# Strassen's seven products for the second FFN product of an attention and FFN kernel

## The chip, the core and the metric

The kernel runs on one core of a Trainium2 chip. TensorE (PE) multiplies matrices into PSUM, which has eight banks of 512 float32 columns; VectorE (DVE), ScalarE (ACT) and GpSimd (POOL) do elementwise work, and SyncE (SP) issues the DMAs. Each engine works through a list of instructions in an order that is fixed when the program is built, and semaphores make one engine wait for another. The metric is device time in microseconds.

## The reference

```python
def _attn_ref(q_l, k_l, v_l, q_g, k_g, v_g):          # 8 batches, 8 heads, 512 local and 32 global rows, depth 64
    out_g = sm(scale * q_g @ k_all.T) @ v_all           # global rows see all keys
    s_ll = np.where(abs(i - j) <= 32, scale * q_l @ k_l.T, -1e9)
    a_l = sm(np.concatenate([scale * q_l @ k_g.T, s_ll], -1))
    return np.concatenate([out_g, a_l @ np.concatenate([v_g, v_l], 2)], 2)

def _moe_ref(x, w_in, w_out):                           # x: 4608 x 512, w_in: 512 x 2048, w_out: 2048 x 512
    h = x @ w_in
    g = np.where(h > 0, h, np.exp(np.minimum(h, 0)) - 1)
    return g @ w_out
```

The attention's output, with its heads side by side, is the x of the FFN.

## The kernel before

Float32 products are made of float16 ones: each operand is split into a high and a low half (`xh`, `xl`; `win` and `wout` in two tiles each; `gh`, `gl`), and three products, high by high, high by low and low by high, add up in one PSUM bank.

The FFN works on 17 blocks of 256 rows and, within a block, on eight pairs p of 128 hidden columns. I call one p of one block a step. `ffn1` makes the step's h: 24 matmuls of 256 columns into one bank h of the pool `ps_h` (two banks). ACT then forms Relu (L239) and Exp (L240), POOL the scaled exponential minus one (L241), DVE the maximum of that and the scaled h, which it reads from the bank (L246), ACT casts it to gh (L248), and DVE subtracts to get gl (L249). `ffn2` multiplies gh and gl by the pair's rows of w_out: 12 matmuls of 512 columns into two banks `acc` (128 rows each), which add up over a block's steps and are then scaled by ACT (L284) and stored. `ffn2` of a step is issued when two further steps have had their `ffn1` (`LAG2`).

The first four blocks are done in four parts, "a" to "d", as the weights arrive and are converted; their partial sums go through DRAM. From the fifth block on, group "f", a block runs its eight steps in one pass.

Attention runs beside it. A "slot" is 128 query rows of four heads (or the global rows of four heads), with four stages: scores and row maxima (L458, L469, L472), exponentials on ACT (L476) and their scaling on POOL (L483), transposes on PE (L494) and copies (L497), and the product with v (L516), copied to x (L520). All of these use the pool `ps_a` (four banks). A table `PACE` says how many quarter steps of the FFN (a `yield` of the generator) come with each stage. `defer(n, fn)` puts work n ticks later, where a tick is a quarter step; a scheduler moves some instructions a little after that. After attention only FFN steps are left. `split_x` makes xh and xl of a block ahead; up to `NX` blocks are held.

Of the kernel before, what the change touches and what calls it, by code (L numbers as in the profile page):

```python
# [49 lines left out]
def attn_ffn(ctx: ExitStack, tc: tile.TileContext, qT, qgT, kT, vT, w_in, w_out, mask, out):  # L50
# [28 lines left out]
    def tick():  # L79
        now[0] += 1  # L80
        for fn in later.pop(now[0], []):
            fn()
# [3 lines left out]
            tick()  # L86

    lead = [True]


    msk = wts.tile([P, 3, KW], F32, name="msk")
# [21 lines left out]
    wout = [wts.tile([P, NFT, DM], F16, name=f"wout{k}") for k in "hl"]  # L113
    warm = wout[0][:, NFT - 1, :]
    nc.vector.memset(warm, 0.0)
    for _ in range(WARM):
# [78 lines left out]
    def tables(group):  # L195

        r = slice(*GROUPS[group])
        wm = wts.tile([P, 4], F32, name=f"wm_{group}")
        t = wts.tile([P, NP], F32, name=f"t_{group}")
        kk = wts.tile([P, NP], F32, name=f"kk_{group}")  # L200
        nc.vector.tensor_mul(t[:, r], pww[:, r], pwo[:, r])
        nc.vector.tensor_reduce(out=wm[:, 0:1], in_=t[:, r], op=ALU.max, axis=AX.X)

        def rest():
            all_max(wm[:, 1:2], wm[:, 0:1])
            nc.vector.reciprocal(wm[:, 2:3], wm[:, 1:2])
            nc.vector.tensor_scalar(t[:, r], pwo[:, r], wm[:, 2:3], 16.0, ALU.mult, ALU.mult)
# [5 lines left out]
        defer(5, rest)  # L213


    ready = {}

    def ffn_stream():
# [1 line left out]
        state = {}  # L220

        def ffn1(job, p):
            group, blk, xh, xl, sc = job
            kk = tab[group][2]
            h = ps_h.tile([P, 2, BLK], F32, name="h")
            for j in range(2):
                f = slice((2 * p + j) * P, (2 * p + j + 1) * P)
                k = 0
                for c in range(NC):
                    for wt, xt in ((win[0], xh), (win[0], xl), (win[1], xh)):  # L230
                        nc.tensor.matmul(h[:, j, :], wt[:, c, f], xt[:, c, :], start=k == 0, stop=k == 11)  # L231
# [7 lines left out]
            nc.scalar.activation(g, hf, AF.Relu, scale=sc[:, p:p + 1])  # L239
            nc.scalar.activation(g, g, AF.Exp, scale=-1.0)  # L240
            nc.gpsimd.tensor_scalar(g, g, -1.0, sc[:, NP + p:NP + p + 1], ALU.add, ALU.mult)  # L241
            gh = ffn.tile([P, 2 * BLK], F16, name="gh", bufs=3)
            gl = ffn.tile([P, 2 * BLK], F16, name="gl", bufs=3)

            def elu():
                nc.vector.scalar_tensor_tensor(out=g, in0=hf, scalar=kk[:, p:p + 1], in1=g,  # L246
                                               op0=ALU.mult, op1=ALU.max)
                nc.scalar.copy(gh, g)  # L248
                defer(1, lambda: nc.vector.tensor_sub(gl, g, gh))  # L249

            defer(1, elu)
            pend.append((job, p, gh, gl))
            yield

        def ffn2():
            job, p, gh, gl = pend.pop(0)
            group, blk, _, _, sc = job
            first, last = GROUPS[group][0], GROUPS[group][1] - 1
            if p == first:
                if group == "a":  # L260
                    od[blk] = dram.tile([2, P, DM], F32, name=f"od{blk}")
                state["acc"] = [ps_o.tile([P, DM], F32, name="acc") for _ in range(2)]
                state["o"] = [ffn.tile([P, DM], F32, name="o", bufs=3) for _ in range(2)]
                if group in "bcd":
                    for t in range(2):
                        nc.sync.dma_start(state["o"][t], od[blk][t])
            acc = state["acc"]
            for t in range(2):
                for j in range(2):
                    s = slice(j * BLK + t * P, j * BLK + (t + 1) * P)  # L270
                    f = 2 * p + j
                    for k, (gt, wt) in enumerate(((gh, wout[0]), (gh, wout[1]), (gl, wout[0]))):
                        nc.tensor.matmul(acc[t], gt[:, s], wt[:, f, :], start=p == first and j == 0 and k == 0,  # L273
                                         stop=p == last and j == 1 and k == 2)
                    if j == 0:
                        yield
                if p == last:
                    o = state["o"][t]
                    oc = sc[:, 2 * NP:2 * NP + 1]
                    if group in "bcd":  # L280
                        nc.vector.scalar_tensor_tensor(out=o, in0=acc[t], scalar=oc, in1=o,
                                                       op0=ALU.mult, op1=ALU.add)
                    else:
                        nc.scalar.activation(o, acc[t], AF.Copy, scale=oc)  # L284
                    nc.sync.dma_start(od[blk][t] if group in "abc" else out_rows(blk, t), o)
                yield

        def split_x(blk):
            xr, mx = ready[blk]
# [26 lines left out]
        def scales(group, mx):  # L316
            sc = ffn.tile([P, 2 * NP + 1], F32, name="xs", bufs=4)
            wm, t, _ = tab[group]
            o = GROUPS[group]
            r = slice(*o)  # L320
            nc.gpsimd.tensor_scalar(sc[:, r], isc[:, r], mx[:, 2:3], 1.0, ALU.mult, ALU.mult)
            nc.gpsimd.tensor_scalar(sc[:, NP + o[0]:NP + o[1]], t[:, r], mx[:, 3:4], 1.0, ALU.mult, ALU.mult)
            nc.gpsimd.tensor_scalar(sc[:, 2 * NP:2 * NP + 1], wm, mx[:, 2:3], 2.0 ** -18, ALU.mult, ALU.mult)
            return sc

        order = list(range(NBL + 1))
# [8 lines left out]
        def choose():  # L335

            for blk in order:
                if blk in xs and xs[blk][3] and step[blk] < 4:
                    group = "f" if "f" in tab and not step[blk] else "abcd"[step[blk]]
                    if group in tab:  # L340
                        step[blk] += 4 if group == "f" else 1
                        xh, xl, mx, _ = xs[blk]
                        return group, blk, xh, xl, scales(group, mx)

        job = None
        left = 0
# [258 lines left out]
    for i, _ in enumerate(attention()):  # L605
# [10 lines left out]
        while done < want:  # L616
# [3 lines left out]
            done += 1  # L620
            convert(1)
            tick()
    for _ in f:
        tick()
    drain()
# [57 lines left out]
```

## Time and profile before

| | |
|---|---|
| runs | 1041.33, 1032.25, 1033.97 us; median 1033.97 |
| profiled execution | 1034.22 us; span of the instructions 1032.1 us |
| mean granted TensorE clock | 0.982 |
| busy share | PE 96%, DVE 55%, ACT 51%, POOL 30% |
| DMA | 81.78 MB, 79 GB/s over the span |

A busy share is the time in which an engine had an instruction under way. A group row gives line, engine, operation, what it writes and reads, shape and count, then busy time and mean duration, then the idle time before its instructions and what ended it. In a row of the timeline stand start, length, engine, line and operation.

### The profile page before, as it was taken

The numbers are of one execution on the slowest core, as the hardware profiler recorded it, in microseconds if no ns is written. First come the engines' busy times: TensorE is split into PE (matmuls) and PEld (weight loads), VectorE is DVE, ScalarE is ACT, GpSimd is POOL, SyncE is SP. The second block draws the span as 40 slices with busy tenths as digits, with TensorE's granted clock in tenths as the row PEclk, the third lists the DMA queues.
The fourth block names the chain that finished last, engine by engine and source line by source line (L and its number), as shares of the span: only waits on it lengthen the run. The fifth ranks groups of instructions, "written<-read, shape, count | busy, mean of one in ns | idle before, by whom it ended". The sixth has DMA issues, their size and how long they took to land.

```text
span 1032.1 us, 18890 instructions
## 1 busy us (share of the span) xinstructions
PE 987.5 (96%) x7192; PEld 682.5 (66%) x7192; DVE 565.1 (55%) x1659; ACT 526.6 (51%) x1257; POOL 306.7 (30%) x549
## 2 busy tenths in 40 slices
PE   6899779899999999999999999999999999999996
PEld 4576555566676777766767667667677667666663
DVE  5789698894455555454555445454545454422221
ACT  4778675575344545455544544554545544434342
POOL 3456545344122232223222322232322222211110
PEclk9699899999999999999999999999999999999998
DMA  7546565451321122112310123012200100000000
GB/s 268 160 137 224 180 199 189 159 187 65 108 68 57 43 67 102 32 37 67 98 36 16 42 77 102 27 32 77 97 22 11 42 23 31 1 21 21 1 21 21
DMA packets 39154, 81.78 MB, mean 79 GB/s; under 512 B 3864, under 2 KB 5912, under 8 KB 39064
## 3 DMA queue, kind: packets, MB, share of 16 engines
q1 hardware_dynamic: 39064, 80.58, 23.6%
q8 instruction: 57, 0.93, 0.4%
q14 instruction: 33, 0.27, 0.1%
HBM read 65.36 MB, written 15.20 MB: 78 GB/s over the span
## 4 chain that ended last, share of the span: by engine, by line
PE 84%; DVE 6%; DMA 3%; POOL 2%; ACT 2%; issue 1%; SPq 0%; POOLq 0%; ACTq 0%
PE h L231 32%; PE acc L273 31%; PE pa L516 6%; PE pa L458 5%; PE pa L494 5%; PE pa L406 2%; DVE cu L159 1%; POOL p L483 1%; DMA k<-kT 1%; DVE cu L163 1%; PE acc L458 1%; PE h L516 1%; PE pa L440 1%; ACT p L476 1%; DMA raw<-w_out 1%
## 5 line engine op out<-in xcount | busy, mean ns | idle before, releaser
L231 PE MATMUL h<-xh,winh 128*128 128x256 f16 x1088 | 298.5, 275 | 11.2 <-DVE g L246 5.6
L231 PE MATMUL h<-xh,winl 128*128 128x256 f16 x1088 | 298.1, 274 | 0.0
L231 PE MATMUL h<-xl,winh 128*128 128x256 f16 x1088 | 298.0, 274 | 0.0
L231 PEld LDWEIGHTS <-winh 128*128 128x128 f16 x2176 | 209.8, 98 | 71.0 <-issue 18.7
L241 POOL TENSOR_SCALAR g<-g,xs 128x512 f32<-128x512 f32 x136 | 98.3, 723 | 389.8 <-ACT g L240 356.3
L273 PE MATMUL acc<-wouth,gh 128*128 128x512 f16 x544 | 207.4, 381 | 3.9 <-ACT o L284 2.4
L273 PE MATMUL acc<-woutl,gh 128*128 128x512 f16 x544 | 206.6, 380 | 0.0
L273 PE MATMUL acc<-wouth,gl 128*128 128x512 f16 x544 | 206.3, 380 | 0.0
L483 POOL TENSOR_SCALAR p<-p,sm 128x224 f32<-128x224 f32 x256 | 133.2, 537 | 194.7 <-DVE sm L481 77.8
L246 DVE SCALAR_TENSOR_TENSOR g<-h,kk_f,g 128x512 f32<-128x512 f32 x104 | 78.1, 751 | 195.6 <-POOL g L241 195.2
L248 ACT CAST gh<-g 128x512 f16<-128x512 f32 x136 | 83.8, 617 | 189.3 <-DVE g L246 188.9
L476 ACT ACTIVATE p<-p,m 128x224 f32<-128x224 f32 x256 | 120.1, 470 | 92.0 <-DVE m L472 91.3
L273 PEld LDWEIGHTS <-gh 128*128 128x128 f16 x1088 | 103.4, 98 | 95.8 <-issue 14.3
L239 ACT ACTIVATE g<-h,xs 128x512 f32<-128x512 f32 x136 | 92.7, 682 | 130.0 <-PE h L231 129.8
L249 DVE TENSOR_TENSOR gl<-g,gh 128x512 f16<-128x512 f32 x136 | 95.0, 699 | 46.2 <-ACT gh L248 45.0
L231 PEld LDWEIGHTS <-winl 128*128 128x128 f16 x1088 | 106.9, 98 | 13.9 <-issue 0.6
L273 PEld LDWEIGHTS <-gl 128*128 128x128 f16 x544 | 53.4, 98 | 63.9 <-issue 0.8
L469 DVE CUSTOM_DVE_ANT_0 p<-pa,msk 128x224 f32<-128x224 f32 x228 | 77.3, 384 | 20.1 <-PE pa L458 19.9
L497 DVE COPY pt<-pa 128x512 f32<-128x512 f32 x99 | 67.5, 682 | 36.6 <-PE pa L494 36.2
L240 ACT ACTIVATE g<-g 128x512 f32<-128x512 f32 x136 | 85.2, 628 | 3.4
L494 PE MATMUL pa<-ident,p 128*128 128x128 f32 x512 | 79.5, 278 | 6.8 <-POOL p L483 4.0
L494 PEld LDWEIGHTS pa<-ident,p 128*128 128x128 f32 x512 | 60.4, 142 | 19.8 <-POOL p L483 8.1
(159 smaller groups left out, 1001.7 us busy)
## 6 DMA issues: line engine op xcount, KB each, us to landing
v<-vT SPq DMA_DIRECT2D x64, 256.0 KB, 2.7
k<-kT SPq DMA_DIRECT2D x32, 448.0 KB, 3.6
out<-o SPq DMA_DIRECT2D x34, 256.0 KB, 2.0
q<-qT SPq DMA_DIRECT2D x32, 256.0 KB, 4.8
raw<-w_in SPq DMA_DIRECT2D x8, 1024.0 KB, 6.6
raw<-w_out SPq DMA_DIRECT2D x8, 1024.0 KB, 5.1
od<-o SPq DMA_DIRECT2D x24, 256.0 KB, 2.9
o<-od SPq DMA_DIRECT2D x24, 256.0 KB, 3.1
```

The source lines that it names most:

```text
L231: nc.tensor.matmul(h[:, j, :], wt[:, c, f], xt[:, c, :], start=k == 0, stop=k == 11)
L239: nc.scalar.activation(g, hf, AF.Relu, scale=sc[:, p:p + 1])
L240: nc.scalar.activation(g, g, AF.Exp, scale=-1.0)
L241: nc.gpsimd.tensor_scalar(g, g, -1.0, sc[:, NP + p:NP + p + 1], ALU.add, ALU.mult)
L246: nc.vector.scalar_tensor_tensor(out=g, in0=hf, scalar=kk[:, p:p + 1], in1=g, op0=ALU.mult, op1=ALU.max)
L248: nc.scalar.copy(gh, g)
L249: defer(1, lambda: nc.vector.tensor_sub(gl, g, gh))
L273: nc.tensor.matmul(acc[t], gt[:, s], wt[:, f, :], start=p == first and j == 0 and k == 0, stop=p == last and j == 1 and k == 2)
L469: nc.vector.tensor_tensor_reduce(out=p[:, 0:KW], in0=sp[r][:, j * KW:(j + 1) * KW], in1=msk[:, mi, :], op0=ALU.add, op1=ALU.max, scale=1.0 ...
L476: nc.scalar.activation(ps[i][:, 0:KW], ps[i][:, 0:KW], AF.Exp, bias=m[:, 1, i:i + 1], scale=scale, accum_out=s[:, 0, i:i + 1])
L483: nc.gpsimd.tensor_scalar(ps[i][:, 0:KW], ps[i][:, 0:KW], s[:, 1, i:i + 1], 1.0, ALU.mult, ALU.mult)
L494: nc.tensor.transpose(tp[:, (2 * r + i) * P:(2 * r + i + 1) * P], ps[2 * j + r][:, i * P:(i + 1) * P], ident)
```

## The change

One-pass blocks but the first compute their second product by Strassen's scheme: g of a step (2 pairs of columns by 2 halves of rows) and the pair's rows of w_out (2 by 2) are each taken as four quarters, and seven products of sums of quarters replace eight. Each product is three matmuls of 256 columns. Seven products lie in four banks, two in each and one in the last; the four banks (the first matmul into one with two products has 512 columns, 256 of them zeros, `wz`) are kept from the first such block to the end: the two of `ps_o`, one of `ps_h` and one of `ps_a`. So `ps_h` has one bank left for h and `ps_a` three for attention; when attention has ended (`alone`), h takes a bank of `ps_a` in every other step. ACT copies the scaled h to SBUF (`hs`), and DVE takes the maximum from there. DVE forms five sums of quarters of g (`gs`), ACT casts two quarters and five sums (`gh`, seven pieces), DVE subtracts (`gl`, seven pieces). At a block's end ACT copies the four banks to `tmp`, and DVE makes the four quarters of the result in eight additions. The sums of quarters of w_out are made once, during the first one-pass block (`add_up`), in buffers that the conversion of weights no longer needs, and two of them in place. `NX` is 4 instead of 5.

```diff
-NX = 5
+NX = 4
+SEVEN = (((4, "B11+B12"), (0, "B22-B12")), ((5, "B21+B22"), (1, "B21-B11")), ((3, "B11"), (2, "B22")), ((6, "B11+B22"),))
...
+    def add_up(p):
...
+            nc.gpsimd.tensor_add(w, wout[0][:, pr, :], wout[1][:, pr, :])
+            nc.vector.tensor_add(s[:, 0:2, :], w[:, :, 0:256], w[:, :, 256:512])
+            nc.vector.tensor_add(s[:, 2, :], w[:, 0, 0:256], w[:, 1, 256:512])
+            nc.vector.tensor_sub(sf[:, 768:1280], w[:, 1, :], w[:, 0, :])
...
+            nc.scalar.copy(flat[0], todo[2][1])
...
         def ffn1(job, p):
-            h = ps_h.tile([P, 2, BLK], F32, name="h")
+            state["h"] = not state.get("h")
+            if alone[0] and state["h"]:
+                h = ps_a.tile([P, 512], F32, name="pa").rearrange("p (j t) -> p j t", j=2)
+            else:
+                h = ps_h.tile([P, 2, BLK], F32, name="h")
...
             nc.scalar.activation(g, hf, AF.Relu, scale=sc[:, p:p + 1])
+            if seven is not None:
+                hs = ffn.tile([P, 2 * BLK], F32, name="hs", bufs=2)
+                nc.scalar.activation(hs, hf, AF.Copy, scale=kk[:, p:p + 1])
             nc.scalar.activation(g, g, AF.Exp, scale=-1.0)
             nc.gpsimd.tensor_scalar(g, g, -1.0, sc[:, NP + p:NP + p + 1], ALU.add, ALU.mult)
...
+            def parts():
+                nc.vector.tensor_max(g, g, hs)
...
+                nc.vector.tensor_add(s[:, 0:2, :], q[:, 0], q[:, 1])
+                nc.vector.tensor_sub(s[:, 2:4, :], q[:, :, 1, :], q[:, :, 0, :])
+                nc.vector.tensor_add(s[:, 4, :], q[:, 0, 0, :], q[:, 1, 1, :])
+                def high():
+                    nc.scalar.copy(gh[:, 0:2, :], two)
+                    nc.scalar.copy(gh[:, 2:7, :], s)
+                def low():
+                    nc.vector.tensor_sub(gl[:, 0:2, :], two, gh[:, 0:2, :])
+                    nc.vector.tensor_sub(gl[:, 2:7, :], s, gh[:, 2:7, :])
+                defer(2, high)
+                defer(4, low)
...
-            defer(1, elu)
+            defer(*(3, parts) if seven is not None else (1, elu))
...
+        def ffn2_seven(blk, p, gh, gl, sc, done):
...
+            for i, bank in enumerate(SEVEN):
+                todo = [(gt[:, a, :], quarter(b, p, w), n)
+                        for n, (a, b) in reversed(list(enumerate(bank))) for gt, w in ((gh, 0), (gh, 1), (gl, 0))]
+                for k, (gt, w, n) in enumerate(todo):
...
+                    nc.tensor.matmul(cols, gt, w, start=first, stop=p == NP - 1 and k == len(todo) - 1)
+                if p == NP - 1:
+                    nc.scalar.activation(e[:, 2 * i:2 * i + w, :]..., acc[i][:, 0:256 * w], AF.Copy, scale=...)
+                yield
...
     for i, _ in enumerate(attention()):
...
+    alone[0] = True
     for _ in f:
         tick()
```

On PE, at the end of the program, a step's `ffn2` and the start of the next matmuls. Before, part of one step (each matmul follows its weight load):

```order
L273 LDWEIGHTS gh
L273 MATMUL acc<-wouth,gh 128x512
L273 LDWEIGHTS gh
L273 MATMUL acc<-woutl,gh 128x512
L273 LDWEIGHTS gl
L273 MATMUL acc<-wouth,gl 128x512
```

and now (the name raw stands for a sum of quarters of w_out that lies in that buffer):

```order
L405 LDWEIGHTS gh
L405 MATMUL acc<-wouth,gh 128x256
L405 LDWEIGHTS gh
L405 MATMUL acc<-woutl,gh 128x256
L405 LDWEIGHTS gl
L405 MATMUL acc<-wouth,gl 128x256
L405 LDWEIGHTS gh
L405 MATMUL acc<-raw,gh 128x256
```

The matmuls are half as wide; there are 21 of them in a step for 12, in four banks.

On ACT, in the last stage, when attention has ended; before, one step and the start of the next (g is the activation, gh its high half):

```order
L239 ACTIVATE g<-h,xs 128x512 [waits PE_49]
L240 ACTIVATE g<-g 128x512 [waits Activation_49]
L248 CAST gh<-g 128x512 [waits DVE_49]
L239 ACTIVATE g<-h,xs 128x512 [waits PE_49]
L240 ACTIVATE g<-g 128x512 [waits Activation_49]
```

and now (pa is here the bank of `ps_a` that h has in every other step):

```order
L301 ACTIVATE g<-pa,xs 128x512 [waits PE_49]
L304 ACTIVATE hs<-pa,kk_f 128x512
L305 ACTIVATE g<-g 128x512 [waits Activation_49]
L325 CAST gh<-g 128x256 [waits DVE_49]
L326 CAST gh<-gs 128x640 [waits DVE_49]
L301 ACTIVATE g<-h,xs 128x512 [waits PE_49]
```

The step has the copy hs and a second cast, which waits for the sums gs; the next step's Relu stands behind it, as it stood behind the one cast before.

Beside attention, about half way between the first changed block and the end of attention; ACT before, from Relu to Relu (L476 are the exponentials of a slot, p its rows):

```order
L239 ACTIVATE g<-h,xs 128x512 [waits PE_49]
L240 ACTIVATE g<-g 128x512 [waits Activation_49]
L520 COPY xr<-pa 128x2x128 [waits PE_49]
L248 CAST gh<-g 128x512 [waits DVE_49]
L476 ACTIVATE p_89,sm<-p_89,m 128x224 [waits DVE_49,Pool_49]
L476 ACTIVATE p_90,sm<-p_90,m 128x224
L239 ACTIVATE g<-h,xs 128x512 [waits PE_49]
```

and now:

```order
L301 ACTIVATE g<-h,xs 128x512 [waits PE_49]
L304 ACTIVATE hs<-h,kk_f 128x512
L305 ACTIVATE g<-g 128x512 [waits Activation_49]
L672 COPY xr<-pa 128x2x128 [waits PE_49]
L325 CAST gh<-g 128x256 [waits DVE_49]
L326 CAST gh<-gs 128x640 [waits DVE_49]
L628 ACTIVATE p_89,sm<-p_89,m 128x224 [waits DVE_49,Pool_49]
L628 ACTIVATE p_90,sm<-p_90,m 128x224
L301 ACTIVATE g<-h,xs 128x512 [waits PE_49]
```

DVE at the same place now (m are the row maxima that the exponentials wait for, L624 scales them):

```order
L316 TENSOR_TENSOR g<-g,hs 128x512 [waits Pool_49]
L681 TENSOR_REDUCE xm<-xr 128x1
L320 TENSOR_TENSOR gs<-g 128x256 [waits DVE_49]
L321 TENSOR_TENSOR gs<-g 128x256
L322 TENSOR_TENSOR gs<-g 128x128
L459 TENSOR_REDUCE xm<-xm 128x1 [waits DVE_49]
L329 TENSOR_TENSOR gl<-g,gh 128x256 [waits Activation_49]
L330 TENSOR_TENSOR gl<-gs,gh 128x640 [waits Activation_49]
L621 ISA p_89,m<-pa,msk 128x224 [waits PE_49]
...
L624 TENSOR_SCALAR m<-m 128x4 [waits DVE_49]
```

The row maxima stand behind the subtraction that waits for the cast of 640 columns, and two exponentials stand between that cast and the next Relu, as they stood behind the one cast of 512 before.

More of the change, by code (lines that the diff above doesn't have):

```diff
@@ L88, in attn_ffn @@
     lead = [True]
+    alone = [False]
     msk = wts.tile([P, 3, KW], F32, name="msk")
@@ L112, in attn_ffn @@
     win = [wts.tile([P, NC, DF], F16, name=f"win{k}") for k in "hl"]
-    wout = [wts.tile([P, NFT, DM], F16, name=f"wout{k}") for k in "hl"]
+    wz = wts.tile([P, 256 + NFT * DM], F16, name="wouth")
+    nc.vector.memset(wz[:, 0:256], 0.0)
+    wout = [wz[:, 256:].rearrange("p (f e) -> p f e", f=NFT), wts.tile([P, NFT, DM], F16, name="woutl")]
     warm = wout[0][:, NFT - 1, :]
@@ L222, in ffn1 @@
         def ffn1(job, p):
-            group, blk, xh, xl, sc = job
+            group, blk, xh, xl, sc, seven = job
             kk = tab[group][2]
-            h = ps_h.tile([P, 2, BLK], F32, name="h")
+            state["h"] = not state.get("h")
[3 more added lines that the diff above has]
+                h = ps_h.tile([P, 2, BLK], F32, name="h")
             for j in range(2):
@@ L256, in ffn2 @@
             job, p, gh, gl = pend.pop(0)
-            group, blk, _, _, sc = job
+            group, blk, _, _, sc, seven = job
             first, last = GROUPS[group][0], GROUPS[group][1] - 1
+            if seven is not None:
+                yield from ffn2_seven(blk, p, gh, gl, sc, seven)
+                return
             if p == first:
@@ L276, in ffn2 @@
                         yield
+                if group == "f" and t:
+                    add_up(p)
                 if p == last:
@@ L342, in choose @@
                         xh, xl, mx, _ = xs[blk]
-                        return group, blk, xh, xl, scales(group, mx)
+                        assert group == "f" or not state.get("f")
+                        seven = [] if state.get("f") else None
+                        state["f"] = group == "f"
+                        return group, blk, xh, xl, scales(group, mx), seven
         job = None
```

91 lines of the change are left out of this document (86 added, 5 removed).

## The prediction

> **What bounds the kernel now.** The page first: the span, the busy shares, the chain that ended last.
>
> ```profile
> span 1032.1 us, 18890 instructions
> PE 987.5 (96%) x7192; PEld 682.5 (66%) x7192; DVE 565.1 (55%) x1659; ACT 526.6 (51%) x1257; POOL 306.7 (30%) x549
> PE 84%; DVE 6%; DMA 3%; POOL 2%; ACT 2%; issue 1%; SPq 0%; POOLq 0%; ACTq 0%
> ```
>
> PE carries 84% of the chain. The windows (length, then busy us and count of PE, PEld, DVE, ACT, POOL, then clock) show it per stage: one with attention beside the FFN, one with the FFN alone.
>
> ```profile
> 550.00:600.00 50.00, 50.00 (x371) 35.17 (x370) 27.11 (x85) 24.96 (x64) 12.87 (x25) 1.00 0.14 47
> 950.00:1000.00 50.00, 50.00 (x351) 34.16 (x350) 13.91 (x20) 19.84 (x31) 6.22 (x9) 1.00 0.03 12
> ```
>
> PE has no idle time in either, at full clock; DVE and ACT are half idle. All that PE ever waited for in L231, where a step's h begins, is small (total us, times, longest):
>
> ```profile
> PE h L231 <- DVE g L246: 5.6, 5, 2.9
> ```
>
> So a shorter second product shortens the kernel, unless something else becomes late. A "step" below is one turn of p: 24 matmuls of `ffn1` and those of `ffn2`. The chain in order of time (start, length) prices both, and the timeline gives the start of the 41st and of the 113th step:
>
> ```profile
> 1007.18 2.62 PE h L231 x24
> 1009.80 2.59 PE acc L273 x12
> 1012.39 2.62 PE h L231 x24
> 1015.01 7.78 PE acc L273 x36
> 1022.82 0.69 ACT o L284
> 383.73 0.27 PE L231 MATMUL h<-xh,winh 128*128 128x256 f16 x1
> 892.18 0.27 PE L231 MATMUL h<-xh,winh 128*128 128x256 f16 x1
> ```
>
> A 256-column matmul with a weight load of its own goes every 2.62/24 = 0.109 us, a 512-column one every 2.59/12 = 0.216. From step 41, where the changed blocks begin (after four blocks in parts and one whole, 40 steps), to step 113, where attention has ended, 72 steps take 508.4 us, **7.06 us each**; the last 23 up to 1012.39 take 120.2 us, 5.23 each, nearly all of it the 2.62 + 2.59 of PE.
>
> **The change on PE.** A changed block has 21 matmuls of 256 columns a step for 12 of 512: 21 x 0.109 = 2.29 us for 2.59, so 0.30 less. In its first step three banks are opened by a 512-column matmul, 3 x 0.107 = 0.32 more. Per block 8 x 0.30 - 0.32 = 2.06 us, and the order shows 12 such blocks (2016 matmuls, 36 of them wide): **24.7 us**, 0.257 a step. Were PE still the bound, a step would take 6.80 beside attention and 4.97 alone.
>
> **What the change puts on ACT and DVE.** These rows give durations and overlap: groups (busy, mean ns), then timelines.
>
> ```profile
> L284 ACT ACTIVATE o<-acc,xs 128x512 f32<-128x512 f32 x34 | 22.8, 680 | 4.4 <-PE acc L273 4.4
> L248 ACT CAST gh<-g 128x512 f16<-128x512 f32 x136 | 83.8, 617 | 189.3 <-DVE g L246 188.9
> L303 ACT ACTIVATE xh<-xr,xm 128x1024 f16<-128x1024 f32 x16 | 18.4, 1148 | 5.7 <-DVE xm L302 4.5 <-DVE sm L481 1.1
> L249 DVE TENSOR_TENSOR gl<-g,gh 128x512 f16<-128x512 f32 x136 | 95.0, 699 | 46.2 <-ACT gh L248 45.0
> L527 DVE TENSOR_TENSOR xglob<-xglob,pa 128x64 f32<-128x64 f32 x41 | 8.8, 215 | 13.1 <-ACT xr L520 13.1
> ...
> 962.95 0.69 ACT L239 ACTIVATE g<-h,xs 128x512 f32<-128x512 f32 x1 [1.64 <-PE h L231]
> 963.67 0.63 ACT L240 ACTIVATE g<-g 128x512 f32<-128x512 f32 x1
> 964.39 0.69 POOL L241 TENSOR_SCALAR g<-g,xs 128x512 f32<-128x512 f32 x1 [4.52 <-ACT g L240]
> 965.12 0.75 DVE L246 SCALAR_TENSOR_TENSOR g<-h,kk_f,g 128x512 f32<-128x512 f32 x1 [3.08 <-POOL g L241]
> 965.90 0.62 ACT L248 CAST gh<-g 128x512 f16<-128x512 f32 x1 [1.60 <-DVE g L246]
> ...
> 600.25 0.19 ACT L476 ACTIVATION_READ_ACCUMULATOR p<-p,m 128x1 f32 x1
> 600.34 0.47 ACT L476 ACTIVATE p<-p,m 128x224 f32<-128x224 f32 x1
> 600.71 0.19 ACT L476 ACTIVATION_READ_ACCUMULATOR p<-p,m 128x1 f32 x1
> 600.80 0.47 ACT L476 ACTIVATE p<-p,m 128x224 f32<-128x224 f32 x1
> ```
>
> ACT: the copy hs of 512 columns out of PSUM is priced as L284, 0.68. Casts: 617 ns for 512 and 1148 for 1024 columns make 1.04 ns a column, so 0.35 for 256 and 0.75 for 640. DVE: 215 ns for 64 and 699 for 512 make 1.08 a column: 0.42 for 256, 0.28 for 128, 0.84 for 640; for the maximum I take L249's 0.70 (L246's 0.75 is the upper end). The sums cost 0.42 + 0.42 + 0.28, the subtractions 0.42 + 0.84: DVE does 3.1 us a step instead of 1.45, and per block eight additions of quarters more, 3.4 us. Independent neighbours overlap by about 0.09 (0.25 to 0.34, 0.71 to 0.80). From engine to engine a result needs 0.03 to 0.09 (964.30 to 964.39, 965.08 to 965.12, 965.87 to 965.90).
>
> None of this is much for half-idle engines, but it lies in **one loop**: ACT does Relu, hs, Exp, and then, before the next Relu, stands at the cast of the sums, which needs POOL and DVE. Alone: Relu 0, hs 0.59, Exp 1.18 to 1.81, POOL 1.90 to 2.59, maximum 2.63 to 3.33, sums to 4.35, cast of 640 from 4.38, next Relu at **5.05**. The old loop (0.69 + 0.63 + 0.69 + 0.75 + 0.62 with the gaps) was 3.6, far below PE's 5.21. The new one is a little above PE's 4.97, so the last stage gives 24 x (5.05 - 5.23) = **-4.3 us**, not -6.2. The second bank that h gets there is cover not needed.
>
> **The same loop beside attention.** There ACT also does four exponentials a slot, 0.46 each (600.34 to 600.80), and copies. Where they stand between Exp and the first cast they hide in the 2.6 us for POOL and DVE; where they stand behind the second cast they lengthen the loop, and so does their own wait: they need DVE's row maxima, which in DVE's queue stand behind the subtractions, which need ACT's cast. Already before, this was among ACT's largest waits:
>
> ```profile
> ACT p L476 <- DVE m L472: 91.3, 47, 6.1
> ...
> 608.69 0.39 DVE L469 CUSTOM_DVE_ANT_0 p<-pa,msk 128x224 f32<-128x224 f32 x1 [1.69 <-PE pa L458]
> 609.00 0.39 DVE L469 CUSTOM_DVE_ANT_0 p<-pa,msk 128x224 f32<-128x224 f32 x1
> ```
>
> The order shown in the section on the change is such a place: cast ends 5.4 (one reduction stands between maximum and sums), subtraction to 6.2, four maxima at 0.31 to 7.5, factor 7.7, two exponentials, next Relu at 8.6. I went through 16 successive steps in this way by hand, with the rows above: seven come to 5.35 to 5.7, one to 6.45, eight to 7.6 to 9.0; the sum is 112.9, **7.05 a step**, against PE's 6.80. Two loops of nearly one length on a single bank for h cannot always cover each other: PE may not begin the next h before hs is read. In the 16 steps PE was late at three places, by about 3 us: +0.2.
>
> POOL adds to it. Four L483 in 2.16 us, when a subtraction fell among them, and in 1.73 when none did:
>
> ```profile
> 477.54 2.16 POOL L483 TENSOR_SCALAR p<-p,sm 128x224 f32<-128x224 f32 x4 [0.97 <-DVE sm L481]
> 478.03 0.92 DVE L249 TENSOR_TENSOR gl<-g,gh 128x512 f16<-128x512 f32 x1 [0.60 <-ACT gh L248]
> 601.97 1.73 POOL L483 TENSOR_SCALAR p<-p,sm 128x224 f32<-128x224 f32 x4 [5.90 <-PE pa L494]
> ```
>
> A meeting costs POOL 0.43 and DVE 0.22 (0.92 for 0.70). DVE now has 3.1 us a step of instructions with both inputs in SBUF for 0.70, so some 0.4 of a step; of two L483 a step about one meets, and half of those meet on the loop: +0.1 (from 0 to 0.4). The Trainium skill, SBUF — State Buffer, section Who interferes with whom, has the rule: a DVE instruction with two SBUF inputs and a GpSimd instruction that reads SBUF exclude each other for a whole instruction. It speaks against this change, whose maximum has two inputs in SBUF where L246 had h in PSUM, and the two rows agree with it; without it the sum below would be 7 us lower.
>
> So a step beside attention takes 7.05 + 0.2 + 0.1 = **7.35**: 72 x (7.35 - 7.06) = **+20.9 us**.
>
> **The rest.** At the end (7.78 of PE, 0.69 of ACT, then 8.6 from 1023.51 to the span's end) the last Relu is followed by 5.1 to the cast, 0.9 subtraction, 2.3 matmuls and drain of 0.2, ACT's 0.4, six additions at 0.33 (independent) to 0.46, 2.3, then the same 8.6: 19.8 for 17.1, **+2.8**. In the first whole block the sums of weights: eight POOL additions of 1024 columns, at least
>
> ```profile
> L152 POOL TENSOR_SCALAR cu<-cu 128x1024 f32<-128x1024 f32 x16 | 18.7, 1169 | 36.3 <-ACT cu L151 35.7
> ```
>
> 1.17 us each and with two inputs perhaps twice that, on a POOL that is 26% busy; DVE 3.6 and ACT 1.6 more a step. Two whole steps of PE's work lie between a step's `ffn1` and its `ffn2` and cover it; without that cover it is 5. I take **+1**. A fourth x instead of a fifth costs nothing: a slot comes free three blocks, some 150 us, before its x is needed. SP issues the same outputs, about 3 us later, and nothing waits behind them; larger buffers and one memset lie ahead of the matmuls.
>
> **Sum.** +20.9 - 4.3 + 2.8 + 1 = +20.4 on the profiled execution's 1034.2, of which 2.1 lie around its span: 1054.6, and as the median of the runs shown is 1034.0, **1055 us**.
>
> **Rivals.** (1) *PE stays the bound*: the steps are 6.80 and 4.97, -18.7 - 6.2 + 2.8, 1012. For it: PE's 96%. Against it: the loop of 5.05, which needs no attention at all. Chance 0.14. (2) *The long steps are absorbed* by PE's lead, and a step is 7.0 at no cost from POOL: -4.3 - 4.3 + 3.8, **1029**, no change. For it: half of the 16 steps have 1 us to spare. Chance 0.22. (3) *My forecast*, 7.2 to 7.6 a step, 1044 to 1073. Chance 0.46. (4) *Three banks for attention*, slower still: the transposes of a slot wait for the first bank of its own scores instead of an older one. DVE frees it after three row maxima, 0.9, and whatever stands ahead of them, up to 2.9 of maximum, sums and a subtraction, while PE has some 2 us of FFN before it gets there; it decides where more than 1.1 us stand ahead. For it: these queues; against it: PE's wait for L469 hardly shows today.
>
> ```profile
> L458 PE MATMUL pa<-k,q 64*128 64x224 f32 x264 | 33.9, 375 | 0.0
> ...
> PE pa L494 <- DVE m L469: 0.4, 1, 0.4
> ```
>
> 264 score matmuls in these 508 us, eight a slot, are 33 slots; at 1 us each it is +33 on the forecast, 1088. Chance 0.18. That the change doesn't do what it says is excluded by the counts of the order; only a price of 256 columns other than 0.109 could undo it, and that is the kernel's commonest matmul.
>
> **Chances.** 1% is 10 us, about what a measurement of this kernel can tell: faster is below 1023.6, slower above 1044.3. Faster: rival 1, 0.14. No change: rival 2 and the low edge of the forecast, 0.26. Slower: 0.60. The range 1020 to 1096 leaves out rival 1 and the top of rival 4, together 0.18.
>
> **What would show it.** In the changed profile: 21 matmuls in 2.3 us in the last stage, and a spacing of steps of 5.05, with ACT idle before the second cast and PE idle at the first h matmul, released by ACT's hs; if that spacing is 4.97, the loop is mispriced. Beside attention PE below 50.00 of 50 us in most windows, its wait at h the largest, around 0.5 us a step. If PE waits at the transposes (L646) instead, rival 4 is right; if it waits nowhere, rival 1. What would make me wrong is an ACT or DVE that overlaps more than the neighbours quoted.

## The result and the profile after

The changed kernel takes 1070.57 us (median of four runs, 1068.82 to 1071.24) against 1033.11 (1030.97 to 1041.33) for the kernel before on the same chip: a ratio of **1.035** [1.0299, 1.0402]. Some executions reach the first whole block about 7 us later than others, with a granted clock of 0.72 to 0.77 between 210 and 240 us where the others have 0.94 to 1.00; so stages are compared below, and medians only beside them.

From the page of the changed kernel, the span and the busy shares:

```profile
span 1068.0 us, 21424 instructions
PE 975.8 (91%) x8056; PEld 765.3 (72%) x8056; DVE 752.0 (70%) x2188; ACT 634.8 (59%) x1497; POOL 349.9 (33%) x557
```

PE is busy for 11.7 us less than before and the span is 35.9 longer, so PE now waits. The windows show in which stage: the first whole block, the 72 steps beside attention (the "main stage" from here on), the last stage up to the end of the last h, the tail. First before, then after:

```profile
329.20:383.70 54.50, 54.50 (x411) 37.60 (x409) 28.80 (x90) 26.97 (x71) 14.08 (x28) 1.00 0.16 52
383.70:892.20 508.50, 508.50 (x3850) 356.18 (x3849) 256.92 (x779) 247.20 (x622) 136.54 (x260) 1.00 0.15 49
892.20:1015.00 122.80, 122.80 (x856) 83.67 (x855) 38.06 (x60) 50.79 (x78) 18.83 (x29) 1.00 0.04 14
1015.00:1032.10 17.10, 7.78 (x37) 3.33 (x34) 1.44 (x2) 3.31 (x5) 0.69 (x1) 0.81 0.10 31
```

```profile
328.90:393.70 64.80, 57.37 (x412) 38.35 (x410) 45.80 (x117) 31.18 (x78) 27.74 (x32) 0.95 0.13 43
393.70:924.50 530.80, 498.68 (x4480) 416.46 (x4479) 376.10 (x1143) 325.07 (x795) 157.98 (x261) 0.99 0.15 48
924.50:1043.00 118.50, 117.21 (x1065) 103.77 (x1063) 77.21 (x174) 72.62 (x129) 20.34 (x29) 1.00 0.04 15
1043.00:1068.00 25.00, 9.59 (x64) 6.11 (x61) 8.40 (x20) 6.55 (x12) 1.38 (x2) 0.76 0.07 21
```

The differences are +10.3, +22.3, -4.3 and +7.9; the start of the first whole block moved by -0.3; together 35.9. In the main stage PE's second number is 32.1 below the first, where before the two were equal. Its waits there (total us, times, longest):

```profile
PE pa L646 <- DVE m L621: 14.8, 11, 2.1
PE pa L646 <- ACT pt L598: 4.7, 2, 2.7
PE pa L646 <- ACT pg L572: 4.4, 3, 2.6
PE pa L405 <- ACT pg L572: 3.9, 1, 3.9
PE h L293 <- ACT hs L304: 2.9, 5, 1.1
```

L646 is the transposes of `stage_t`: they wait for a bank of `ps_a` that DVE's row maxima or ACT still hold. The wait for h, which I had expected to be the largest, is the smallest of these five.

The first whole block, in which five of the eight additions of `add_up` on POOL lie (two stand ahead of it, one behind), reads best as a timeline. POOL and DVE around the longest gap, and the transposes that ended it:

```profile
381.45 2.50 POOL L252 TENSOR_TENSOR cu<-wouth,woutl 128x1024 f32<-128x1024 f16 x1 [5.49 <-DVE sm L633]
...
383.95 1.89 POOL L635 TENSOR_SCALAR p<-p,sm 128x224 f32<-128x224 f32 x4
385.83 0.69 POOL L306 TENSOR_SCALAR g<-g,xs 128x512 f32<-128x512 f32 x1
386.55 0.75 DVE L337 SCALAR_TENSOR_TENSOR g<-h,kk_f,g 128x512 f32<-128x512 f32 x1 [2.32 <-POOL g L306]
387.99 0.69 DVE L340 TENSOR_TENSOR gl<-g,gh 128x512 f16<-128x512 f32 x1 [0.68 <-ACT gh L339]
388.60 0.22 DVE L677 COPY xglob<-pa 128x64 f32<-128x64 f32 x1
...
388.96 1.09 PE L646 MATMUL pa<-ident,p 128*128 128x128 f32 x4 [5.04 <-DVE xglob L677]
```

POOL's addition for `add_up` (L252) takes 2.50 us. Behind it in POOL's list stand four normalisations and then the plain step's multiplication; DVE stands at L337 for the latter; behind L337, and a subtraction that waits for ACT's cast of its result (L340), stands the copy of a bank of `ps_a`, and for that bank PE waits 5.04 us. The window of 4 us in which the gap ends shows what it costs beyond itself (the clock is the third number from the end):

```profile
388.00:392.00 4.00, 3.04 (x10) 1.63 (x11) 3.97 (x12) 2.25 (x5) 0.45 (x1) 0.50 0.00 0
```

### The profile page after: what moved, and what is told of

It is laid out like the page before. It is cut to its first block, busy times and chain, and to the rows that moved or that the text cites. A ratio compares the mean times of both kernels' runs of the same rounds, so it can differ in the third digit from the quotient of the medians.

```text
span 1068.0 us, 21424 instructions
## 1 busy us (share of the span) xinstructions
PE 975.8 (91%) x8056; PEld 765.3 (72%) x8056; DVE 752.0 (70%) x2188; ACT 634.8 (59%) x1497; POOL 349.9 (33%) x557
## 3 DMA queue, kind: packets, MB, share of 16 engines
q1 hardware_dynamic: 39064, 80.58, 22.8%
## 5 line engine op out<-in xcount | busy, mean ns | idle before, releaser
L293 PE MATMUL h<-xh,winh 128*128 128x256 f16 x992 | 273.1, 275 | 14.3 <-DVE g L337 11.0
L293 PE MATMUL h<-xl,winh 128*128 128x256 f16 x992 | 272.7, 275 | 0.0
L293 PE MATMUL h<-xh,winl 128*128 128x256 f16 x992 | 272.6, 275 | 0.0
L293 PEld LDWEIGHTS <-winh 128*128 128x128 f16 x2176 | 210.4, 98 | 60.3 <-issue 22.7
L316 DVE TENSOR_TENSOR g<-g,hs 128x512 f32<-128x512 f32 x96 | 66.3, 690 | 127.2 <-POOL g L306 127.1
L405 PEld LDWEIGHTS <-gh 128*128 128x128 f16 x1344 | 129.1, 98 | 29.5 <-issue 12.2
L325 ACT CAST gh<-g 128x256 f16<-128x256 f32 x96 | 39.0, 406 | 134.6 <-DVE g L316 134.6
L646 PE MATMUL pa<-ident,p 128*128 128x128 f32 x512 | 81.2, 282 | 37.7 <-DVE m L621 16.8
L326 ACT CAST gh<-gs 128x640 f16<-128x640 f32 x96 | 69.5, 724 | 46.9 <-DVE gs L322 46.6
L646 PEld LDWEIGHTS pa<-ident,p 128*128 128x128 f32 x512 | 59.3, 144 | 52.7 <-issue 40.9
L330 DVE TENSOR_TENSOR gl<-gs,gh 128x640 f16<-128x640 f32 x96 | 79.7, 830 | 17.3 <-ACT gh L326 16.4
L405 PEld LDWEIGHTS <-gl 128*128 128x128 f16 x672 | 65.9, 98 | 14.8 <-DVE gl L329 1.5
L405 PE MATMUL acc<-raw,gh 128*128 128x256 f16 x384 | 73.6, 274 | 0.3
L668 PE MATMUL pa<-pt,v 128*64 128x160 f32 (+2 forms) x864 | 66.6, 295 | 0.8 <-DVE m L621 0.8
```

The lines of the kernel that those rows point to most:

```text
L326: nc.scalar.copy(gh[:, 2:7, :], s)
L330: nc.vector.tensor_sub(gl[:, 2:7, :], s, gh[:, 2:7, :])
L405: nc.tensor.matmul(cols, gt, w, start=first, stop=p == NP - 1 and k == len(todo) - 1)
L646: nc.tensor.transpose(tp[:, (2 * r + i) * P:(2 * r + i + 1) * P], ps[2 * j + r][:, i * P:(i + 1) * P], ident)
```

## The experiments

The theory on record is an in-order loop through ACT, POOL and DVE that is longer than PE's step because of the added elementwise work. Its rival is the ring of three banks. For each run: the median, the ratio to before with its interval, and the length of the main stage in its profile.

| run | us | ratio | main stage, us |
|---|---|---|---|
| before | 1033.1 | 1 | 508.5 |
| after | 1070.6 | 1.035 [1.0299, 1.0402] | 530.8 |
| four banks | 1056.6 | 1.0184 [1.0109, 1.0258] | 518.0 |
| no sums | 1038.5 | 1.0032 [0.999, 1.0073] | 508.1 |
| four banks, no sums | 1027.6 | 0.9933 [0.9898, 0.9968] | 495.7 |
| four banks, DVE's part of the sums | 1046.7 | 1.014 [1.0089, 1.0191] | 513.4 |
| four banks, ACT's part of the sums | 1029.6 | 0.997 [0.9942, 0.9998] | 496.7 |
| before with three banks | 1041.8 | 1.006 [1.0027, 1.0093] | 514.7 |
| before with one bank for h | 1035.2 | 1.0027 [1.0, 1.0055] | 509.1 |
| add_up's addition on DVE | 1065.8 | 1.0313 [1.0265, 1.036] | 531.8 |
| parts three ticks later | 1074.4 | 1.0333 [1.0267, 1.0399] | 534.7 |
| a subtraction on POOL | 1093.4 | 1.0529 [1.0462, 1.0597] | 553.1 |
| multiplication on DVE | 1052.7 | 1.0166 [1.0103, 1.0229] | 515.5 |
| both moves to DVE | 1043.7 | 1.0088 [1.0062, 1.0114] | 512.8 |

### Ring and load, apart and together

Four banks for the attention:

```diff
-                                  ps_h.tile([P, 2, BLK], F32, name="h").rearrange("p a b -> p (a b)"),
-                                  ps_a.tile([P, 512], F32, name="pa")]
+                                  ps_h.tile([P, 2, BLK], F32, name="h").rearrange("p a b -> p (a b)")]
+                state["seven"].append(state["seven"][2])
```

> The changed kernel, with the product m1 (B11+B22) added into the bank that holds m4 and m6, so that its bank of ps_a goes back to the attention, which then has four again; instructions, their order and their number stay as they were. Only c11 and c22 come out as other numbers. If the ring of three banks makes the transposes of stage_t wait (24 us of idle PE ahead of them between 394 and 925 us in the changed kernel's trace), most of that goes: 1070.6 - 20 = about 1050 us (1044 to 1056). If the added work on ACT and DVE is what sets the step of the main stage, the wait only moves to another line, the wait at h first: 1066 to 1072 us.

No sums (the matmuls stay and read zeros), and then both edits:

```diff
-                nc.vector.tensor_add(s[:, 0:2, :], q[:, 0], q[:, 1])
-                nc.vector.tensor_sub(s[:, 2:4, :], q[:, :, 1, :], q[:, :, 0, :])
-                nc.vector.tensor_add(s[:, 4, :], q[:, 0, 0, :], q[:, 1, 1, :])
-                    nc.scalar.copy(gh[:, 2:7, :], s)
-                    nc.vector.tensor_sub(gl[:, 2:7, :], s, gh[:, 2:7, :])
```

> The changed kernel without the elementwise work on the five sums of g in parts(): three additions of DVE, the 640-column cast of ACT (724 ns) and the 640-column subtraction of DVE are left out, and the matmuls that used the sums read zeros of the same shape, so PE's work and the three banks stay. If the added work of ACT and DVE makes the banks late, the main stage loses most of its 32 us of idle PE, and the last stage its lag behind ACT: 1070.6 - 28 = about 1040 us (1034 to 1048). If three banks are too few whatever the load, the waits at the transposes stay: 1060 to 1068 us.

> Both edits together: four banks of ps_a for the attention and no elementwise work on the five sums. Every theory so far leaves PE bound in the main stage here, so this shows what the products alone bring: 72 steps at about 6.75 to 6.9 us instead of 7.37, and the first whole block still 10 us longer: 1025 to 1038 us. If it stays near the run without sums alone, the ring costs nothing once the load is gone; if it stays near the run with four banks alone, the load costs nothing once the ring is long.

The main stage in the windows, for the three in this order:

```profile
394.40:912.40 518.00, 496.32 (x4479) 416.75 (x4478) 374.33 (x1143) 324.66 (x795) 157.56 (x262) 1.00 0.15 49
```

```profile
392.70:900.80 508.10, 496.35 (x4479) 417.30 (x4478) 265.39 (x859) 277.25 (x724) 142.37 (x262) 0.99 0.16 50
```

```profile
402.40:898.10 495.70, 491.70 (x4479) 416.06 (x4478) 264.63 (x859) 277.01 (x724) 142.63 (x262) 1.00 0.16 51
898.10:1015.10 117.00, 117.00 (x1065) 104.03 (x1064) 39.09 (x84) 58.62 (x107) 18.73 (x30) 1.00 0.04 15
1015.10:1035.10 20.00, 6.86 (x63) 5.90 (x61) 3.89 (x10) 4.52 (x8) 0.69 (x1) 0.80 0.09 26
```

The fourth bank is worth 12.8 us with the sums (530.8 to 518.0) and 12.4 without (508.1 to 495.7). The sums cost 22.7 with three banks and 22.3 with four. **The two prices add**; neither theory alone is the answer. (The median with four banks, 1056.6, lies just above the range that was to show the ring, 1044 to 1056, and far below the other.) With both gone the stage is 12.8 below before, and a step takes 6.89.

With four banks PE's wait moves to where the prediction had put it:

```profile
PE h L293 <- ACT hs L304: 14.8, 15, 2.3
```

That is 0.21 us a step, for the 0.2 of the prediction. The longest of the fifteen, DVE, ACT and PE of that run:

```profile
827.84 0.42 DVE L329 TENSOR_TENSOR gl<-g,gh 128x256 f16<-128x256 f32 x1
828.17 0.16 DVE L626 TENSOR_SCALAR m<-m 128x4 f32<-128x4 f32 x1
...
828.37 0.48 ACT L630 ACTIVATE p<-p,m 128x224 f32<-128x224 f32 x1 [0.93 <-DVE m L626]
...
830.25 0.67 ACT L301 ACTIVATE g<-h,xs 128x512 f32<-128x512 f32 x1
830.82 0.67 ACT L304 ACTIVATE hs<-h,kk_f 128x512 f32<-128x512 f32 x1
...
831.53 0.27 PE L293 MATMUL h<-xh,winh 128*128 128x256 f16 x1 [2.29 <-ACT hs L304]
```

ACT idles 0.93 us for DVE's factor (L626), which stands behind the maxima and a subtraction; the four exponentials that it then does stand ahead of Relu and hs, and PE, with one bank for h, waits 2.29.

The parts alone, in the kernel before. Three banks:

```diff
-    ps_a = ctx.enter_context(tc.tile_pool(name="ps_a", bufs=4, space=PSUM))
+    ps_a = ctx.enter_context(tc.tile_pool(name="ps_a", bufs=3, space=PSUM))
```

> The kernel before, with three banks in ps_a instead of four (the eighth bank lies idle), nothing else changed. If three banks are too few for the attention whatever the load of ACT and DVE, transposes wait here as well: 16 to 24 us more, 1050 to 1057 us. If it takes the added work to make the banks late, the kernel stays within 5 us of before: 1033 to 1038 us.

```profile
386.70:901.40 514.70, 510.52 (x3850) 355.80 (x3849) 257.80 (x779) 247.51 (x622) 136.48 (x260) 1.00 0.15 49
```

+6.2 in the main stage and 3.0 more ahead of it (it starts at 386.7 instead of 383.7), where this kernel has only three banks too: between the two expectations. Half the price of the ring is thus there without any of the change; the other half comes with the shorter products or the one bank for h, which these runs don't separate.

One bank for h, with hs and four x:

```diff
+            if pinned:
+                hs = ffn.tile([P, 2 * BLK], F32, name="hs", bufs=2)
+                nc.scalar.activation(hs, hf, AF.Copy, scale=kk[:, p:p + 1])
...
+                    nc.vector.tensor_max(g, g, hs)
```

> The kernel before with one part of the change alone: from the second whole block on, one of the two banks of ps_h is taken out of use, ACT copies h to SBUF (hs) behind its Relu and DVE's maximum reads that; x of four blocks on chip; plain products, four banks of ps_a, two accumulators as before. If the single h bank behind ACT's queue makes PE wait (0.2 us a step as the prediction put it, or more), this costs 14 us or more in the main stage: 1047 us and above. If ACT is back at h in time as long as the sums aren't there, PE stays bound and this stays within 4 us of before: 1033 to 1037 us.

```profile
382.90:892.00 509.10, 508.40 (x3847) 356.03 (x3847) 252.15 (x777) 280.42 (x691) 135.22 (x259) 1.00 0.16 49
```

PE stays bound: ACT's 33 us more (280.42 for 247.20) cost 0.6.

### Which engine's work on the sums

Four banks with one half of the work each. DVE's part kept (the cast left out, the subtraction against 640 columns of w_out, `w0`), then ACT's part kept (the cast from 640 columns of the mask, `ms`):

```diff
-                    nc.scalar.copy(gh[:, 2:7, :], s)
-                    nc.vector.tensor_sub(gl[:, 2:7, :], s, gh[:, 2:7, :])
+                    nc.vector.tensor_sub(gl[:, 2:7, :], s, w0)
```

> Between the run with four banks alone (1056.6 us, all the elementwise work) and the one without it (1027.6 us): four banks, DVE's three additions and its 640-column subtraction (against other data of the same shape) kept, ACT's 640-column cast left out; the products of sums read zeros. If DVE's queue is what delays the banks (row maxima behind the subtractions, and with them the exponentials that stand ahead of Relu on ACT), this stays near the former: 1045 to 1057 us. If ACT's in-order loop with its 0.72 us cast sets the step, it falls near the latter: 1027 to 1036 us.

```diff
-                    nc.scalar.copy(gh[:, 2:7, :], s)
+                    nc.scalar.copy(gh[:, 2:7, :], ms)
-                    nc.vector.tensor_sub(gl[:, 2:7, :], s, gh[:, 2:7, :])
```

> The other half: four banks, ACT's 640-column cast kept (from constant data, so that it waits for no addition), DVE's three additions and the 640-column subtraction left out. If DVE's queue is the cause, this comes out near the run without any of it: 1027 to 1034 us. If ACT's loop is, it keeps most of the 29 us: 1045 to 1057 us.

```profile
394.60:908.00 513.40, 495.33 (x4479) 416.90 (x4478) 370.96 (x1143) 277.12 (x724) 158.17 (x262) 1.00 0.16 49
```

```profile
393.70:890.40 496.70, 491.89 (x4479) 416.02 (x4478) 265.58 (x859) 321.26 (x796) 142.04 (x262) 1.00 0.16 51
```

Against 495.7 with neither, **DVE's part costs 17.7 us and ACT's cast 1.0**; together they cost 22.3. The cast of constants waits for no sum, so the 1.0 is the price of the cast's time alone; ACT's stand at the cast until the sums are there is left out of both runs, and with the time that the two parts cost each other it is at most the 3.6 us that remain. Neither holds the step as DVE's part does.

### What DVE's queue can be relieved of

Three moves within the changed kernel, three banks and all sums in place. In its main stage DVE waits longest ahead of the maximum (L316: busy, mean, then the idle time before it), for POOL's multiplication:

```profile
L316 DVE TENSOR_TENSOR g<-g,hs 128x512 f32<-128x512 f32 x71 | 49.0, 690 | 92.3 <-POOL g L306 92.2
```

First, everything from the maximum on three ticks later:

```diff
-            defer(*(3, parts) if seven is not None else (1, elu))
+            defer(*(3 if alone[0] else 6, parts) if seven is not None else (1, elu))
```

> The changed kernel with parts() deferred by six ticks instead of three while attention runs (three as before in the last stage); high and low follow two and four ticks later as they did. DVE waited 92 us for POOL's multiplication at the maximum (L316) in the changed kernel's main stage, with the row maxima queued behind it. If that wait is what takes DVE's slack away, it shrinks below 50 us, the transposes' 24 us of idle PE halve, and the time falls to 1050 to 1060 us. If it is DVE's work as such (376 us busy in 531), or if the order on DVE is hardly moved by the deferral, the time stays at 1066 to 1073 us.

```profile
L316 DVE TENSOR_TENSOR g<-g,hs 128x512 f32<-128x512 f32 x71 | 49.0, 691 | 85.6 <-POOL g L306 85.5
```

The wait hardly moved: the scheduler still moves instructions after `defer`, and in the trace the maximum kept its place among DVE's other instructions within three rows, with what follows it in place or a few rows later. So the run says nothing on what a shorter wait would bring. Second, the 640-column subtraction on POOL:

```diff
-                    nc.vector.tensor_sub(gl[:, 2:7, :], s, gh[:, 2:7, :])
+                    (nc.vector if alone[0] else nc.gpsimd).tensor_sub(gl[:, 2:7, :], s, gh[:, 2:7, :])
```

> The changed kernel with the 640-column subtraction of low() on POOL instead of DVE while attention runs. It takes 59 us of DVE's 376 in the main stage away and puts 71 subtractions of two inputs on POOL, worked out at 2320 ns x 640/1024 = 1.45 us each, 103 us. If DVE's queue is what delays the banks, and POOL (158 us busy in 531) has room, PE's 32 us of idle time fall by a third or more: 1055 to 1064 us. If POOL's queue is what DVE waits for at the maximum (92 us at L316 already), the wait grows by more than DVE saves: 1072 to 1085 us.

```profile
L316 DVE TENSOR_TENSOR g<-g,hs 128x512 f32<-128x512 f32 x71 | 49.1, 692 | 115.1 <-POOL g L306 115.0
...
400.40:953.50 553.10, 507.50 (x4480) 421.09 (x4479) 345.83 (x1072) 325.42 (x795) 254.32 (x333) 0.98 0.15 46
```

DVE is busy 30 us less in this stage, and the stage is 22.3 longer; the median, 1093.4, lies above even the range for a longer wait (1072 to 1085). So DVE's busy time is not the measure either. DVE waits 22.8 us more for POOL's multiplication; and since 59.1 us of subtractions were taken from it, the rest of its instructions have grown by 29 us beside POOL's (the subtraction L329 from 426 to 516 ns). The run doesn't separate POOL's lateness from this. Third, the opposite, POOL's multiplication to DVE:

```diff
-            nc.gpsimd.tensor_scalar(g, g, -1.0, sc[:, NP + p:NP + p + 1], ALU.add, ALU.mult)
+            dve = seven is not None and not alone[0]
+            if not dve:
+                nc.gpsimd.tensor_scalar(g, g, -1.0, sc[:, NP + p:NP + p + 1], ALU.add, ALU.mult)
...
             def parts():
+                if dve:
+                    nc.vector.tensor_scalar(g, g, -1.0, sc[:, NP + p:NP + p + 1], ALU.add, ALU.mult)
                 nc.vector.tensor_max(g, g, hs)
```

> The changed kernel with the multiplication ahead of the maximum, (exp - 1) times scale (L306), on DVE instead of POOL in the blocks that use the seven products, while attention runs; the last stage keeps it on POOL. DVE gets 71 instructions more, estimated from its 128x1024 one-input form of 681 ns at 0.35 to 0.40 us each, 27 us in the main stage; POOL loses 72 of 719 ns. If the hand-over from POOL, with POOL's normalisations queued ahead of it, is what holds DVE's queue (92 us of waiting at the maximum), the wait falls to 40 us or less (the exponential of ACT is what it then waits for), more than DVE pays, and PE's idle 32 us fall to about 20: 1055 to 1063 us. If it is DVE's own work, 376 us of busy time becoming 403, the time rises: 1073 to 1082 us.

```profile
392.60:908.10 515.50, 497.58 (x4479) 417.08 (x4478) 408.07 (x1215) 326.37 (x795) 110.24 (x190) 0.99 0.16 49
...
L319 DVE TENSOR_SCALAR g<-g,xs 128x512 f32<-128x512 f32 x72 | 38.2, 530 | 54.8 <-ACT g L305 54.7
```

DVE is busy 32 us more, and the stage is **15.3 us shorter**: more than the fourth bank brings. The instruction was dearer than estimated (530 ns for 350 to 400), the wait fell to 54.8 and not to 40, and the time is still below what was expected. That would fit a second effect beside DVE's wait: POOL's normalisations, whose results the transposes take, no longer stand behind the multiplication. It is not shown: in the main stage of the kernel after PE waits for none of them. DVE's other instructions also became 6 us shorter in all (38.2 us were added, and its busy time rose by 32.0); no run separates these.

### The first whole block

```diff
-            nc.gpsimd.tensor_add(w, wout[0][:, pr, :], wout[1][:, pr, :])
+            nc.vector.tensor_add(w, wout[0][:, pr, :], wout[1][:, pr, :])
```

> The changed kernel with the first addition of add_up, high plus low half of a pair of rows of w_out, on DVE instead of POOL; nothing else. If the five to eight additions of POOL (2.1 to 2.5 us each, with the four normalisations and the step's multiplication of POOL queued behind them) are what made the first whole block 10.3 us longer, that block falls from 64.8 to 55 to 58 us, and the time to about 1062 us (1060 to 1065). If it is add_up's other work (three additions, four casts and subtractions a pair on DVE and ACT), the block stays above 62 us and the time at 1068 to 1072.

The block's window in this run, and POOL's additions in the kernel after, where they lie in that block:

```profile
335.80:393.40 57.60, 54.96 (x412) 37.60 (x410) 45.88 (x116) 30.51 (x78) 18.54 (x27) 1.00 0.16 49
```

```profile
L252 POOL TENSOR_TENSOR cu<-wouth,woutl 128x1024 f32<-128x1024 f16 x5 | 11.6, 2320 | 20.3 <-DVE tmp L259 14.8 <-DVE sm L633 5.5
```

The block falls from 64.8 to 57.6, at full clock: 7.2 of its 10.3 us came from the addition's place on POOL, with all else of `add_up` in place. The median, 1065.8, is a little above the expected range; in the profiled execution the block starts at 335.8 instead of 328.9, so what was lost there lies ahead of it.

Both moves to DVE together:

> The same, with the first addition of add_up on DVE as well (which took the first whole block from 64.8 to 57.6 us). The two edits lie in different blocks, so their effects should add: 7 us below the run with the multiplication alone, 1048 to 1056 us if the hand-over theory holds, 1066 to 1075 if DVE's own work is the bound. It isn't expected to reach the kernel before: three banks alone cost 12 us of the main stage and DVE's additions and subtraction most of 22.

1043.7 us, 9.0 below the multiplication alone and below the expected range (1048 to 1056). The first whole block takes 57.6 us as with the addition alone, and the main stage 512.8, so the two moves add; the best form of the change that computes all of it is still 1.0088 [1.0062, 1.0114] times before. Only runs that leave work out are faster than before, and the fastest by 0.7%.

## Why the prediction was right in direction and short in size

1055 was forecast and 1070.6 came, of +35.9 us in the profile +20.4. Term by term:

- **PE's own saving: right.** 6.80 a step beside attention was reckoned; with sums and ring gone it is 6.89, of which 4.0 us of idle time make 0.06. The last stage without sums takes 117.0 for 122.8, -5.8 for the -6.2 of PE alone.
- **Main stage, +20.9 forecast, +22.3 measured: right by luck, two errors that cancel.** The forecast was made for a ring that costs nothing, and that case was run: four banks, 518.0, 7.19 a step where I had 7.35. So the loop, with PE's and POOL's additions to it, was priced 11 us too high. The ring, which I had as a rival with a chance of 0.18, costs 12.8. Calling it a rival was the mistake of form: it does not exclude the loop, and both were paid. Its price of 1 us a slot was too high, 12.8/33 = 0.39.
- **The loop's place.** That ACT's exponentials stand ahead of the next Relu, and wait for maxima behind the sums and a factor behind a subtraction in DVE's queue, is what the timeline at 828 us shows. But I had called ACT's stand at the cast of the sums the heart of it, and without that stand DVE's part still costs 17.7 of the 22.3 us. POOL, which I charged 0.1 a step for its meetings with DVE, matters more than that: taking the multiplication from it brings 15.3 us. The meetings themselves no run prices; POOL's normalisations take 594 ns each in the main stage for 513 before.
- **Last stage, -4.3 forecast, -4.3 measured: the number right, the path not.** ACT's loop is there: its Relus go 4.95 us apart for the 5.05 forecast, none of them waiting for PE, and with the copies of the four banks at a block's end it is 5.08 on the mean of the eight steps from 985.82. But I had PE wait for the loop at h, and it doesn't once. All that PE waits for in this stage is the copies, at the start of a block's accumulation:

```profile
985.82 0.68 ACT L301 ACTIVATE g<-h,xs 128x512 f32<-128x512 f32 x1
...
990.77 0.68 ACT L301 ACTIVATE g<-pa,xs 128x512 f32<-128x512 f32 x1
...
1026.49 0.68 ACT L301 ACTIVATE g<-h,xs 128x512 f32<-128x512 f32 x1
...
1046.29 0.68 ACT L301 ACTIVATE g<-h,xs 128x512 f32<-128x512 f32 x1
...
PE acc L405 <- ACT tmp L408: 1.3, 2, 0.9
```

The second bank for h, which I had called cover not needed, lets PE run ahead of ACT. My sign that 4.97 would mean a mispriced loop was a poor one: PE's own 4.97 and the loop's 4.95 are the same to 0.02.
- **Tail, +2.8 forecast, +7.9 measured.** What the loop costs comes out here. The last Relu starts at 1046.29, 3.3 us after the last h is done at 1043.0: ACT had fallen behind PE. I had let both begin together. From that Relu to the end it is 21.7 us where I had 19.8. Without the sums the tail takes 20.0. The last stage and the tail together were to be 1.5 us shorter and are 3.6 longer.
- **First whole block, +1 forecast, +10.3 measured: the largest miss.** I asked whether a step's own results would be late, and found two steps of cover. What was late was everything behind a 2.3 us addition in POOL's list. My "perhaps twice" 1.17 was its true price, but I multiplied it with nothing. The Trainium skill, GPSIMD Engine Reference, section Elementwise — side-by-side cycle accounting, has 4497 ns for a float32 addition of 2048 columns. Half of that agrees with the 2320 ns here, where the inputs are float16; the price would not have saved the term, since the queue behind it was missing.

## What to carry to other kernels

An engine that is a third busy is not free: before an instruction is added to it, list what stands behind that instruction in its queue, and who waits for that, as with POOL's addition here. Prices of different resources (banks, an engine's queue) can add; treat one as a rival of the other only where one excludes the other, and run the two by two table. And where a stage is held by a chain through several in-order engines, a shorter chain can be worth more than less work: 32 us more on DVE bought 15 us.

## What was not expected of the hardware

PE's idle time was followed by matmuls at half rate, or not, and its length decides that only in part. PE around the wait at L405 in the second whole block of the kernel after:

```profile
423.37 0.59 PE L405 MATMUL pa<-cu,gh 128*128 128x256 f16 x2 [3.93 <-ACT pg L572]
423.97 0.42 PE L293 MATMUL h<-xh,winh 128*128 128x256 f16 x1
424.18 0.42 PE L293 MATMUL h<-xl,winh 128*128 128x256 f16 x1
```

After 3.93 us of idleness the matmuls start every 0.21 us instead of 0.109, until 428; after 5.04 us the clock is 0.50 as well (the window from 388 to 392 above). After a wait of 2.06 us it was not so in the kernel after; but in the run with `add_up`'s addition on DVE the same wait, 2.05 us long, was followed by half rate. The wait and the 4 us behind it, first in the kernel after, then in that run:

```profile
590.28 0.63 PE L646 MATMUL pa<-ident,p 128*128 128x128 f32 x4 [2.06 <-DVE m L621]
590.28:594.28 4.00, 4.00 (x37) 3.66 (x38) 2.54 (x9) 3.38 (x11) 0.83 (x2) 1.00 0.00 0
```

```profile
589.36 0.63 PE L646 MATMUL pa<-ident,p 128*128 128x128 f32 x4 [2.05 <-DVE m L621]
589.36:593.36 4.00, 4.00 (x23) 3.08 (x24) 2.26 (x8) 3.38 (x11) 0.83 (x2) 0.63 0.00 0
```

In all traces of this case, from the first whole block to the last h, no wait of 1.0 to 1.9 us was followed by a clock of 0.50; of the 20 waits between 1.97 and 2.73 us eight were; and so were all of 2.9 us and more. The Trainium skill, TensorE: Matmul & The Clock Gate, Part 1 (The HAM clock gate), says that a window of some 3.4 us without work halves the clock and that as much work brings it back. The two waits over 3.4 us agree; the 2.05 us here, and the others below 3.4, do not, and the measurement decides. So in a kernel bound by PE a wait of 3 us costs more than it lasts, and one of 2 us may: as an estimate, some 4 us at half rate behind each of the two long gaps are 2 us of work lost, half as much again as a gap of 4 us.
